# A cosine-gated MLP behind normalised linear attention: second batch's kv in one block on 128 partitions, leftover rows in 32-column tiles, g as a row, a new order

## The chip, the cores and the metric

The kernel runs on one core of one Trainium2 chip. The time is device time of one launch, in microseconds; three launches were timed and the median is used. One further execution was recorded by the hardware profiler, and the profile and trace come from it. The engines are TensorE (PE, matmuls), VectorE (DVE), ScalarE (ACT), GpSimd (POOL) and SyncE (SP, which here only issues DMAs).

## The reference

```python
# q, k, v: (8 batches, 8 heads, 576, 64); w_in: (512, 2048), w_out: (2048, 512) in float64
kv  = np.einsum('bhsd,bhse->bhde', k, v)
out = np.einsum('bhsd,bhde->bhse', q, kv)
rms = np.sqrt(np.mean(out * out, axis=-1, keepdims=True) + 1e-06)
x   = (out / rms * g_norm)          # then to (4608 tokens, 512): heads side by side
h   = x @ w_in
g   = h * np.cos(h)
y   = (g @ w_out).astype(np.float32)
```

The attention has no softmax, so each head's k and v shrink to one 64x64 matrix kv, and each token's q is multiplied by it. The bulk of the work is the two matrix products of the MLP.

## The kernel before

**Chunks and steps.** The 4608 tokens are cut into nine chunks of 512. A batch has 576 tokens, so the second chunk (c = 1) holds the last 64 tokens of batch 0, the "leftover rows", and 448 of batch 1. The inner width of 2048 is cut into 16 pieces j. A step is a chunk and a j: stage 1 (`stage1_part`) makes h for 128 of the 2048 columns, `act_part` makes g from it on ACT and DVE, stage 2 (`stage2_part`) adds g times a piece of w_out to four accumulators. Stage 1 takes the four head pairs p = 0 to 3 of x in this order, three matmuls for each. Every fp32 value is split into a high and a low part (`xhi`, `xlo`; `ghi`, `glo`; the two halves of a weight tile), and three products stand for one; so a step has 12 matmuls of 128x512 in stage 1 and 12 in stage 2, and there are 9 x 16 = 144 steps. The first steps alternate between the first two chunks (`segments`, line 256), so that each weight is used twice soon after its arrival: steps 0 to 3 are chunk 0, 4 to 11 chunk 1.

**Weights.** `w_loads` (line 429) fetches a piece of w_in or w_out as 64-bit words, 512 KB each; `w_part` (line 698) turns it into two fp32 tiles with two or three ACT and three or four DVE operations.

**The front.** The first two batches (`FRONT = 2`) have a path of their own. `kv_loads_front` (line 376) loads k and v of one pair of heads: for batch 0 as 64 rows per head, both heads on 128 partitions, for batch 1 on 96 partitions with six tokens each. `kv_front_part` (line 452) multiplies them on PE, one pair at a time, and copies the 64x64 results into the block-diagonal tile `kv_front`. `q_loads_front` (line 410) loads q of one pair; `x_front_part` (line 531) transposes it on PE, multiplies it by `kv_front`, squares (ACT), sums (DVE), takes the power -0.5 on POOL, scales (DVE), transposes back on PE, and makes `xhi` (ACT, scaled by `gcol`, the column of g) and `xlo` (DVE). For chunk 1 each pair does six products (lines 558 to 563): four on 128 rows of batch 1, of which the first two cover rows that are not batch 1's, and two of 32 columns that overwrite those rows with the leftover rows of batch 0. Later batches use `kv_part` (line 494): all four pairs in one block, with four full tiles of 128 tokens and the last 64 tokens (`k_over`, `v_over`, zero-filled to 128) as a fifth product.

**g.** Line 391 loads g as a column of 64 partitions, four bytes each, on ACT's queue; `g_part` (line 354) copies it to the other 64.

**The order.** A planner written out in the kernel (`Order`, line 52) sets the order on every engine. Each piece of work is a generator that waits for events, takes tokens (buffers) and asks for time on an engine with a cost and a priority. The planner walks through time and takes the piece that can start first, and among those the one with the lowest priority value; `keep_in_program_order` fixes what comes out. The priorities are due times, `due(i) = 24 + 5.4 i + 2 min(i, 11)`, shifted by a table `haste` (line 274). Loads are such pieces on an engine "DMA" (`load`, line 339), and their order is the order in which SP issues them.

**Borrowed memory.** The front's tiles use the names of weight tiles (`lend`, line 889), so in the trace a front load of k reads `wi<-in_k_dram` or `wo<-in_k_dram`, and a kv product `bank<-wo,wi`. The products of q are `acc<-wo,m` (chunk 0) and `bank<-wo,m` (chunk 1). The weights whose tiles are lent wait for the release.

**Start-up.** Lines 240 and 241 issue 34 matmuls on a tile of zeros, before any data has come.

All engine instructions but a few carry line 207 in the trace, since they go through the `Pinned` helper; so they are told apart by their tiles.

Of the kernel before, what the change touches and what calls it, by code (L numbers as in the profile page):

```python
# [51 lines left out]
class Order:  # L52
# [23 lines left out]
    def advance(self, proc, value):  # L76
        while True:
            try:
                req = proc.gen.send(value)
            except StopIteration:  # L80
                self.live.discard(proc)
                return
            value = None
            self.seq += 1
            if req[0] == "run":
                proc.shape = req[3] if len(req) > 3 else None
                self.pending.append((req[2], self.seq, proc.t, req[1], proc))
                return
            if req[0] == "wait":
                proc.t = max([proc.t] + [e.t for e in req[1] if e.t is not None])  # L90
                proc.left = [e for e in req[1] if e.t is None]
                if proc.left:
                    for e in proc.left:
                        e.waiters.append(proc)
                    return
            else:
                tokens = req[1]
                if not tokens.free:
                    heapq.heappush(tokens.waiters, (req[2] if len(req) > 2 else -100.0, self.seq, proc))
# [27 lines left out]
    def run(self):  # L127
        while self.pending:
# [15 lines left out]
            if e == "PE":  # L144

                d = (2 * d if start < 6 else d) + (self.CHANGE if proc.shape != self.shape else 0)
                self.shape = proc.shape
# [7 lines left out]
def tile_kernel(  # L155
# [25 lines left out]

    FRONT = 2
    SF = 2 * S // P
    SP = 96
    SQ = S // SP

# [10 lines left out]
    sched.busy["DMA"] = 1.0  # L197
# [42 lines left out]
    for _ in range(34):  # L240
        pe.matmul(out=bank[:, 0:P], lhsT=zeros, rhs=zeros, start=True, stop=True)
    ident = const.tile([P, P], F32, name="ident")
# [8 lines left out]
    for t in (k_over, v_over):  # L251
        pool.memset(t[ST:P], 0.0)
    gcol = const.tile([P, 1], F32, name="gcol")
# [15 lines left out]
    def due(i):  # L269
# [14 lines left out]
        ("act", 16): 16.2, ("act", 29): 32.0, ("act", 35): 63.7, ("act", 4): -10, ("act", 5): -8.1,  # L284
        ("act", 8): 10.6, ("acc", 0): 28.7, ("acc", 1): 19.9, ("acc", 10): 20.7, ("acc", 13): 59.2,
        ("acc", 14): 44.4, ("acc", 18): 32.3, ("acc", 26): 10.6, ("acc", 28): 15.6, ("acc", 33): 25.2,
        ("acc", 46): 5.6, ("acc", 53): 6.8, ("acc", 8): 12.3, ("xd", 2, 0): -3.8, ("xd", 2, 2): -11.8,
        ("xd", 2, 3): -24.5, ("xd", 3, 0): -12.5,
# [33 lines left out]
    g_in, over_in = Event(), events(B)  # L322
# [28 lines left out]
    def load_g():  # L351
        pass

    def g_part():
        yield "wait", [g_in]
        yield "run", [("ACT", 0.1)], -11.0
        act.copy(out=gcol[D:2 * D, :], in_=gcol[0:D, :])

# [16 lines left out]

    def kv_loads_front(b, p, tags):

        def issue():
            shape = [P, 2, SQ, D] if b else [P, SF, D]
            kv_tiles[b, p] = [wpool.tile(shape, F32, name=f"{kind}{j}") for kind, j in tags]  # L380
            for t, src in zip(kv_tiles[b, p], (k, v)):
                heads = src[b, 2 * p:2 * p + 2]

                queue = nc.sync if b or p else act
                if b:
                    queue.dma_start(out=t[0:SP], in_=heads.rearrange("h (p i) d -> p h i d", i=SQ))  # L386
                else:
                    queue.dma_start(out=t, in_=heads.rearrange("h (p i) d -> (h p) i d", i=SF))
            if not b and not p:
                act.activation(out=warm, in_=warm, func=AF.Sin)  # L390
                act.dma_start(out=gcol[0:D, :], in_=g_norm.rearrange("(d o) -> d o", o=1))
# [18 lines left out]
    def q_loads_front(c, p, tag):  # L410

        def issue():
            if tag not in q_fronts:
                q_fronts[tag] = wpool.tile([P, 4, NTT, D], F32, name=f"{tag[0]}{tag[1]}")
            qn = q_fronts[tag][:, 2 * (p % 2):2 * (p % 2) + 2, :, :]
            heads = slice(2 * p, 2 * p + 2)
# [9 lines left out]
            q_tiles[c, p] = qn  # L426
# [25 lines left out]
    def kv_front_part(b, p, prio):  # L452
# [4 lines left out]
        _, end = yield "run", [("PE", 0.7 if b else 1.05)], prio, D if b else 0  # L457
# [3 lines left out]
        n = SQ if b else SF  # L461
        for i in range(n):
            for j, r in enumerate(heads):
                lhs, rhs = (t[0:SP, j, i, :] if b else t[r, i, :] for t in (kt, vt))
                pe.matmul(out=ps[r, 0:D], lhsT=lhs, rhs=rhs, start=(i == 0), stop=(i == n - 1))
        sched.fire(kv_used[b, p], end)
        done = [Event(), Event()]

# [24 lines left out]

    def kv_part(b, prio):
# [6 lines left out]
        ps = ps_tile(bank)[:, 0:NP * D].rearrange("p (n d) -> p n d", d=D)  # L501
        heads = [slice(j * D, (j + 1) * D) for j in range(2)]
        for p in range(NP):
            kt, vt = kv_tiles.pop((b, p))
            for i in range(SI + 1):
                for j, r in enumerate(heads):
                    lhs, rhs = (
                        (kt[:, j, i, :], vt[:, j, i, :]) if i < SI else (t[:, 2 * p + j, :] for t in (k_over, v_over)))
                    pe.matmul(out=ps[r, p, :], lhsT=lhs, rhs=rhs, start=(i == 0), stop=(i == SI))
            sched.fire(kv_used[b, p], end)  # L510
            sched.give(t_two, end)
        end = yield from kv_parts(b, [ps[r] for r in heads], prio)
# [18 lines left out]
    def x_front_part(c, p, prio):  # L531
# [14 lines left out]
        todo = front_rows(c)  # L546
        yield "wait", [kv_done[b, p] for b in {b for b, _, _, _ in todo}]
# [6 lines left out]
        _, end = yield "run", [("PE", 1.6 if c else 0.95)], prio  # L554
# [3 lines left out]
        for b, r0, r1, m in todo:  # L558
            for j in range(2):
                o = (2 * j + m) * P  # L560
                pe.matmul(
                    out=by_token[r0:r1, 2 * m:2 * m + 2, j, :], lhsT=qT[:, o + r0:o + r1],
                    rhs=kv_front[b][:, 2 * p + j, :], start=True, stop=True)
# [7 lines left out]
        def heads(t):  # L571
# [8 lines left out]
        yield "run", [("POOL", 1.4)], prio  # L580
# [7 lines left out]
            in1=rinv.rearrange("p (n o) -> p n o", o=1).broadcast_to([P, 2 * NTT, D]), op=ALU.mult)  # L588
        _, end = yield "run", [("PE", 0.5)], prio
        for a in range(NTT):  # L590
            pe.transpose(out=ps[:, a * P:(a + 1) * P], in_=x[:, a * P:(a + 1) * P], identity=ident)
        sched.give(t_r, end)
        tokens = x_tokens(c, p)
# [17 lines left out]
    def x_part(c, p, prio):  # L611
# [23 lines left out]
        _, end = yield "run", [("PE", sum(2 * max(0.11, (n + 32) / 2400) for _, _, _, n in parts))], -1.0  # L635
# [62 lines left out]
    def w_part(key, prio):  # L698
# [23 lines left out]
        yield "wait", [low_done]  # L722
        yield "run", [("DVE", 0.69)], prio
# [53 lines left out]
    def act_part(i, h, bank):  # L777
# [11 lines left out]
        sched.give(t_ki, end)  # L789

# [22 lines left out]
    def stage2_part():  # L813
        for i, (c, j, first, final) in enumerate(steps):
            yield "wait", [w_done["wo", j], g_done[i]]
            for t in range(NTT):
# [13 lines left out]
                if final:  # L830
                    sched.spawn(out_part(c, t, accs[t], j == NJ - 1, due(i + 3)), end + 0.1)
# [64 lines left out]
    for b in range(FRONT):  # L896
# [4 lines left out]
        (pool if b else dve).memset(kv_front[b], 0.0)  # L901
    for c in range(FRONT):
        for p in range(NP):
            t = due(begin[c]) - 32 + 3 * p if c else -100.0 + p
            t += put_off("load kv", c, p)
            load(2.4 if c else 1.9, t, [kv_in[c, p]], kv_loads_front(c, p, lend(2, [kv_used[c, p]])))
            if p in (0, 2):
                [key] = lend(1, [q_used[c, p], q_used[c, p + 1]])
            t += put_off("load q", c, p)
            load(1.1 if c else 0.85, t, [q_in[c, p]], q_loads_front(c, p, key))  # L910
            if c == 0 and p == 1:
                load(0.5, t, [g_in], load_g)
                sched.spawn(g_part())
    for c in range(FRONT):
        for p in range(NP):
            t = due(begin[c]) - 24 + 1 * p if c else -10.0 + 0.5 * p
            sched.spawn(kv_front_part(c, p, t + put_off("kv", c, p)))
            sched.spawn(x_front_part(c, p, t + put_off("x", c, p)))
    for key in sorted(need, key=lambda x: (need[x], x)):
        t = due(need[key]) - 14.0 + put_off("load", *key)  # L920
        load(1.5, t, [w_in[key]], w_loads(key), wait=lent.get(key, ()))
# [11 lines left out]
    for b in range(FRONT, B):  # L933
        i, _ = window(chunks_of(b)[0])
        begun = gates[max(i - LEAD, last_step[0] + 1)]
        load(0.8, due(i) - 6.0, [over_in[b,]], over_loads(b), wait=[begun] + ([kv_used[b - 1, NP - 1]] if b > FRONT else []))
# [44 lines left out]
```

## Time and profile before

| | |
|---|---|
| median of three runs | 860.79 us (859.9 to 862.53) |
| the profiled execution | 862.48 us, span 860.7 us |
| PE idle in the span | 9.9 us |
| main matmuls (128x512) | 3456 of 4458 records on PE |
| DMA moved | 59.52 MB; 47.19 MB read from HBM, 11.53 MB written |
| loads of batch 1's k and v | 8 of 288 KB |
| loads of chunk 1's q | 12 (128, 96 and 32 KB for each pair) |

The span runs from the first to the last instruction; the execution's own time also holds what lies around it. A row of the timeline gives start, length, engine, line, operation, out<-in by the program's names, the shape of the stationary operand and of the moving one, and the number of records merged into the row. A fp32 matmul leaves two records. "PEld" is the loading of the stationary operand, which runs beside the matmuls. A window row gives the busy time of the engines within a stretch.

### The profile page before, as it was taken

How to read it: one execution, taken by the hardware profiler on the slowest of the kernel's cores; microseconds unless marked ns; L12 is line 12 of the kernel's file. 1: busy time of each engine (PE TensorE's matmuls, PEld its weight loads, DVE VectorE, ACT ScalarE, POOL GpSimd, SP SyncE). 2: the span in 40 equal slices, each digit the busy share in tenths (PEclk: the TensorE clock that was granted, in tenths of full speed). 3: DMA queues.
4: the chain of work that ended last, by engine and by line, in shares of the span. 5: the costliest groups of instructions: out<-in, count | busy, mean ns of one | idle time of the engine just before them, and what ended most of it. 6: DMA issues, size and time to landing. Idle time of an engine off the chain costs nothing.

```text
span 860.7 us, 12112 instructions
## 1 busy us (share of the span) xinstructions
PE 850.8 (99%) x4458; PEld 705.5 (82%) x4458; DVE 651.4 (76%) x1053; ACT 556.7 (65%) x1059; POOL 103.7 (12%) x49
## 2 busy tenths in 40 slices
PE   8899999999999999999999999999999999999998
PEld 7688888888788888888888888888888888888886
DVE  4999988899987757886778667876778678864554
ACT  4788888667666556665666566756666666664443
POOL 3310000013122101111102101210111111110000
PEclk9999999999999999999999999999999999999999
DMA  8996020371403111400223020402000110010001
GB/s 298 265 398 201 2 85 25 108 199 25 111 13 97 26 62 22 113 13 13 65 52 82 1 74 12 115 9 62 13 13 13 47 28 1 1 38 12 1 0 50
DMA packets 104731, 59.52 MB, mean 69 GB/s; under 512 B 69728, under 2 KB 95072, under 8 KB 104672
## 3 DMA queue, kind: packets, MB, share of 16 engines
q1 hardware_dynamic: 104160, 58.02, 23.4%
q8 instruction: 35, 0.57, 0.3%
q10 hardware_dynamic: 512, 0.72, 0.2%
q14 instruction: 24, 0.20, 0.1%
HBM read 47.19 MB, written 11.53 MB: 68 GB/s over the span
## 4 chain that ended last, share of the span: by engine, by line
PE 95%; DMA 3%; SPq 1%; DVE 0%; issue 0%; ACT 0%; DVEq 0%
PE bank L207 50%; PE acc L207 45%; DMA wi<-in_v_dram 2%; DMA wo<-in_k_dram 1%; DVE r L207 0%; SPq L437 0%; SPq L386 0%; SPq L418 0%; ACT r L207 0%; DVE glo L207 0%; DVE slot L207 0%; ACT ki L207 0%; ACT slot L207 0%; DVEq L207 0%
## 5 line engine op out<-in xcount | busy, mean ns | idle before, releaser
L207 PE MATMUL acc<-wo,ghi 128*128 128x512 f32 x1152 | 355.7, 390 | 0.0
L207 PE MATMUL bank<-xhi,wi 128*128 128x512 f32 x1088 | 337.3, 391 | 0.1
L207 PEld LDWEIGHTS acc<-wo,ghi 128*128 128x128 f32 x1152 | 215.7, 188 | 45.2 <-DVE slot L207 0.4
L207 ACT ACTIVATE r<-r 128x512 f32<-128x512 f32 x288 | 181.3, 630 | 94.4 <-DVE r L207 92.0
L207 PEld LDWEIGHTS bank<-xhi,wi 128*128 128x128 f32 x1088 | 202.4, 188 | 41.6 <-DVE wi L207 0.4
L207 PE MATMUL acc<-wo,glo 128*128 128x512 f32 x576 | 224.5, 390 | 0.3 <-DVE glo L207 0.3
L207 PE MATMUL bank<-xlo,wi 128*128 128x512 f32 x544 | 212.1, 390 | 0.1
L207 POOL TENSOR_TENSOR rinv<-ms,mhalf 128x16 f32<-128x16 f32 (+1 forms) x36 | 99.2, 2756 | 651.5 <-DVE ms L207 651.5
L207 DVE SCALAR_TENSOR_TENSOR r<-ki,bank 128x512 f32<-128x512 int32 x144 | 98.7, 686 | 72.1 <-ACT ki L207 70.6
L207 ACT ACTIVATE ki<-bank 128x512 int32<-128x512 f32 x144 | 85.6, 595 | 90.3 <-PE bank L207 86.5
L207 DVE SCALAR_TENSOR_TENSOR r<-r,bank 128x512 f32<-128x512 f32 x144 | 98.3, 683 | 55.1 <-ACT r L207 54.4
L207 PEld LDWEIGHTS acc<-wo,glo 128*128 128x128 f32 x576 | 108.1, 188 | 23.3 <-DVE glo L207 0.7
L207 PEld LDWEIGHTS bank<-xlo,wi 128*128 128x128 f32 x544 | 102.1, 188 | 21.8 <-DVE xlo L207 0.6
L207 ACT CAST ghi<-r 128x512 fp32r<-128x512 f32 x144 | 89.1, 619 | 43.2 <-DVE r L207 40.8
L207 DVE TENSOR_TENSOR glo<-r,ghi 128x512 fp32r<-128x512 f32 x144 | 99.0, 688 | 23.6 <-ACT ghi L207 21.2
L207 DVE SCALAR_TENSOR_TENSOR r<-ki,r 128x512 f32<-128x512 int32 x144 | 98.6, 685 | 1.2
L207 DVE TENSOR_TENSOR slot<-bank,slot 64x512 f32<-64x512 f32 x56 | 38.5, 688 | 19.0 <-ACT slot L207 18.1
L207 ACT COPY slot<-bank 64x512 f32<-64x512 f32 x56 | 32.6, 581 | 21.1 <-PE bank L207 20.2
L207 ACT ACTIVATE slot<-acc 128x512 f32<-128x512 f32 (+1 forms) x39 | 22.5, 592 | 8.8 <-PE acc L207 7.6
L207 ACT COPY swp<-part 32x16 f32<-32x16 f32 x112 | 22.6, 202 | 7.5 <-DVE part L207 5.8
L207 DVE STREAM_TRANSPOSE slot<-rinv 128x512 f32<-128x512 f32 x28 | 19.8, 706 | 4.1 <-POOL rinv L207 4.0
L207 DVE SCALAR_TENSOR_TENSOR sg<-sg,m 128x512 int32<-128x512 int32 x32 | 21.7, 685 | 0.6 <-ACT sg L207 0.6
(94 smaller groups left out, 580.1 us busy)
## 6 DMA issues: line engine op xcount, KB each, us to landing
out_dram<-slot SPq DMA_DIRECT2D x35, 256.0 KB, 2.0
wo<-in_moe_w_out_dram SPq DMA_DIRECT2D x16, 512.0 KB, 8.4
wi<-in_moe_w_in_dram SPq DMA_DIRECT2D x16, 512.0 KB, 8.6
m<-in_k_dram SPq DMA_DIRECT2D x24, 256.0 KB, 3.8
sg<-in_v_dram SPq DMA_DIRECT2D x24, 256.0 KB, 4.4
part<-slot SPq DMA_DIRECT2D x8, 256.0 KB, 5.7
slot<-part SPq DMA_DIRECT2D x8, 256.0 KB, 3.5
qb<-in_q_dram SPq DMA_DIRECT2D x32, 48.0 KB, 2.3
```

Of the source, the lines that this page charges most:

```text
L207: return lambda *a, **kw: tc.keep_in_program_order(f(*a, **kw))
```

## The change

1. **Batch 1's kv** is made by a new part, `kv_batch_part`, once k and v of all four pairs and the leftover rows have come: 128 partitions with four tokens each, the last 64 tokens through `k_over` and `v_over` as in `kv_part`. The four copies are of 64 x 256. `kv_front_part` is left to batch 0.
2. **Chunk 1's products of q**: the first 128 rows are done in eight products of 32 columns (32 rows of the result each), the leftover rows with batch 0's kv and the other three tiles with batch 1's; the other 128 rows in two whole products. So nothing is overwritten.
3. **g** is loaded twice as one row, on SP, with a priority; one PE matmul against a 1x1 of the identity turns it into a column, which ACT copies. The casts of x wait for it.
4. **q of chunk 1** is loaded for two pairs at a time.
5. **The first loads** (k, v and q of pair 0, q of pair 1) are issued at once, outside the planner, whose DMA then starts at 4.8; costs in the planner are new (loads 1.5 and 1.36 instead of 2.4, 1.9 and 1.5; POOL 1.65 instead of 1.4; no double PE time before 6). `haste` is a new table with more entries, and more keys (`kc`, `xn`, `xt`, `wb`, `ag`, `out`) shift priorities within a part. Priorities are rounded to thousandths.
6. **40 start-up matmuls** instead of 34.

```diff
-    for _ in range(34):
+    for _ in range(40):
         pe.matmul(out=bank[:, 0:P], lhsT=zeros, rhs=zeros, start=True, stop=True)
...
-        ("load kv", 0, 0): -15.1, ("load kv", 0, 1): 6.2, ("load kv", 0, 2): 2.5, ("load kv", 0, 3): 3.5,
-        ("load kv", 1, 1): -98.4, ("load kv", 1, 3): 27.5, ("load q", 0, 0): -4.0, ("load q", 0, 1): -28.8,
...
+        ("load kv", 0, 0): -15.1, ("load kv", 0, 1): -32.7, ("load kv", 0, 2): -615.2, ("load kv", 0, 3): -234.6,
+        ("load kv", 1, 0): -254.1, ("load kv", 1, 1): -98.4, ("load kv", 1, 2): -36.0, ("load q", 0, 0): -4.0,
+        ("load q", 0, 1): -28.8, ("load q", 0, 2): -682.5, ("load q", 0, 3): -16.6, ("load q", 1, 0): 209.1,
+        ("load q", 1, 2): 118.1, ("load q", 1, 3): -94.8, ("load", "wi", 0): -465.8, ("load", "wi", 1): -214.2,
...
+        ("load", "wi", 6): 50.8, ("load", "wi", 7): -26.1, ("load", "wo", 0): 10.0, ("load", "wo", 1): -295.7,
...
+    def load_g():
+        for j in range(2):
+            nc.sync.dma_start(out=grow[:, j, :], in_=g_norm.rearrange("(o d) -> o d", o=1))
+
+    def g_part(prio):
...
+        pe.matmul(
+            out=ps[:, 0:1], lhsT=grow.rearrange("o j d -> o (j d)"), rhs=ident[0:1, 0:1], start=True, stop=True)
+        _, end = yield "run", [("ACT", 0.2)], prio
+        act.copy(out=gcol, in_=ps[:, 0:1])
...
-            shape = [P, 2, SQ, D] if b else [P, SF, D]
+            shape = [P, 2, SI, D] if b else [P, SF, D]
...
-                    queue.dma_start(out=t[0:SP], in_=heads.rearrange("h (p i) d -> p h i d", i=SQ))
+                    queue.dma_start(out=t, in_=heads[:, 0:SI * P].rearrange("h (p i) d -> p h i d", i=SI))
...
+            n = 4 if c else 2
+            qn = q_fronts[tag][:, 2 * (p % 2):2 * (p % 2) + n, :, :]
+            heads = slice(2 * p, 2 * p + n)
...
+    def kv_batch_part(b, prio):
+
+        yield "wait", [kv_in[b, p] for p in range(NP)] + [over_in[b,]]
+        yield "take", t_psa, prio
+        bank = yield "take", t_bank, prio
+        _, end = yield "run", [("PE", 0.58 * NP)], prio, D
+        ps = kv_products(b, bank, end)
...
+        def copies(n):
+            j, r = n // 2, halves[n % 2]
+            e, end = yield "run", [("ACT", act_us(NP * D), 0.0), ("DVE", dve_us(NP * D), 0.3)], prio
+            copy(e, front[r, :, j, r], ps[halves[j]])
+            sched.fire(done[n], end)
...
-        todo = front_rows(c)
-        yield "wait", [kv_done[b, p] for b in {b for b, _, _, _ in todo}]
+
+        todo = [(0, P, m, j, c) for m in range(c, 2) for j in range(2)]
+        if c:
+
+
+            n = (S - CH) // 2
+            todo = [(r, r + n, 0, j, c if r else 0) for j in range(2) for r in range(0, P, n)] + todo
+        prio += put_off("xn", c, p)
+        yield "wait", [kv_done[b, p] for b in range(c + 1)]
...
+    at_once = {("kv", 0, 0): 6.8, ("q", 0, 0): 5.2, ("q", 0, 1): 6.8}
...
+                load(1.5, t, [kv_in[c, p]], issue)
+                if c and not p:
+                    load(1.6, t + put_off("load over"), [over_in[c,]], over_loads(c))
```

`kv_products` is the loop of products of `kv_part`, taken out so that both parts call it.

More of the change, by code (lines that the diff above doesn't have):

```diff
@@ L144, in run @@
             if e == "PE":
-                d = (2 * d if start < 6 else d) + (self.CHANGE if proc.shape != self.shape else 0)
+                d += self.CHANGE if proc.shape != self.shape else 0
                 self.shape = proc.shape
@@ L196, in tile_kernel @@
     sched = Order()
-    sched.busy["DMA"] = 1.0
+    sched.busy["DMA"] = 4.8
     class Pinned:
@@ L349, in load @@
         sched.spawn(part())
[L351 to L357, printed above, removed]
     def two(shape, dtype, which):
@@ L425, in issue @@
                         in_=q[b, heads, t:t + 2 * (r1 - r0), :].rearrange("h (r a) d -> r h a d", a=2))
-            q_tiles[c, p] = qn
+            for i in range(0, n, 2):
+                q_tiles[c, p + i // 2] = qn[:, i:i + 2]
         return issue
@@ L456, in kv_front_part @@
         bank = yield "take", t_bank, prio
-        _, end = yield "run", [("PE", 0.7 if b else 1.05)], prio, D if b else 0
+        _, end = yield "run", [("PE", 1.05)], prio, 0
         ps = ps_tile(bank)
@@ L460, in kv_front_part @@
         heads = [slice(j * D, (j + 1) * D) for j in range(2)]
[L461 to L465, printed above, removed]
+        for i in range(SF):
+            for r in heads:
+                pe.matmul(out=ps[r, 0:D], lhsT=kt[r, i, :], rhs=vt[r, i, :], start=(i == 0), stop=(i == SF - 1))
         sched.fire(kv_used[b, p], end)
         done = [Event(), Event()]
+        prio += put_off("kc", b, p)
         def copies(j):
@@ L492, in kv_parts, with kv_products @@
         return end
+    halves = [slice(j * D, (j + 1) * D) for j in range(2)]
+    def kv_products(b, bank, end):
+        ps = ps_tile(bank)[:, 0:NP * D].rearrange("p (n d) -> p n d", d=D)
+        for p in range(NP):
+            kt, vt = kv_tiles.pop((b, p))
+            for i in range(SI + 1):
+                for j, r in enumerate(halves):
+                    lhs, rhs = (
+                        (kt[:, j, i, :], vt[:, j, i, :]) if i < SI else (t[:, 2 * p + j, :] for t in (k_over, v_over)))
+                    pe.matmul(out=ps[r, p, :], lhsT=lhs, rhs=rhs, start=(i == 0), stop=(i == SI))
+            sched.fire(kv_used[b, p], end)
+        return ps
+    def kv_batch_part(b, prio):
+        yield "wait", [kv_in[b, p] for p in range(NP)] + [over_in[b,]]
+        yield "take", t_psa, prio
+        bank = yield "take", t_bank, prio
+        _, end = yield "run", [("PE", 0.58 * NP)], prio, D
+        ps = kv_products(b, bank, end)
+        prio += put_off("kc", b, 0)
+        front = kv_front[b].rearrange("p (n j) d -> p n j d", j=2)
+        done = [Event() for _ in range(4)]
+        def copies(n):
[3 more added lines that the diff above has]
+            sched.fire(done[n], end)
+        for n in range(4):
+            sched.spawn(copies(n), end)
+        yield "wait", done
+        end = max(e.t for e in done)
+        give_ps(bank, end)
+        for p in range(NP):
+            sched.fire(kv_done[b, p], end)
     def kv_part(b, prio):
@@ L500, in kv_part @@
         _, end = yield "run", [("PE", 0.58 * NP)], -1.0, D
[L501 to L510, printed above, removed]
+        ps = kv_products(b, bank, end)
+        for _ in range(NP):
             sched.give(t_two, end)
-        end = yield from kv_parts(b, [ps[r] for r in heads], prio)
+        end = yield from kv_parts(b, [ps[r] for r in halves], prio)
         give_ps(bank, end)
@@ L553, in x_front_part @@
             bank = yield "take", t_bank, prio
-        _, end = yield "run", [("PE", 1.6 if c else 0.95)], prio
+        _, end = yield "run", [("PE", 1.25 if c else 0.95)], prio
         ps = ps_o.tile([P, DM], F32, name=f"acc{acc}") if c == 0 else ps_tile(bank)
         by_token = ps.rearrange("p (a j d) -> p a j d", j=2, d=D)
[L558 to L563, printed above, removed]
+        for r0, r1, m, j, b in todo:
+            o = (2 * j + m) * P
+            pe.matmul(
+                out=by_token[r0:r1, 2 * m:2 * m + 2, j, :], lhsT=qT[:, o + r0:o + r1],
+                rhs=kv_front[b][:, 2 * p + j, :], start=True, stop=True)
         sched.fire(q_used[c, p], end)
@@ L634, in x_part @@
             banks.append((yield "take", t_bank, prio))
-        _, end = yield "run", [("PE", sum(2 * max(0.11, (n + 32) / 2400) for _, _, _, n in parts))], -1.0
+        _, end = yield "run", [("PE", 0.05 + sum(2 * (n + 30) / 2400 for _, _, _, n in parts))], -1.0
         both = [ps_tile(bank) for bank in banks]
@@ L905, in tile_kernel @@
             t += put_off("load kv", c, p)
-            load(2.4 if c else 1.9, t, [kv_in[c, p]], kv_loads_front(c, p, lend(2, [kv_used[c, p]])))
+            issue = kv_loads_front(c, p, lend(2, [kv_used[c, p]]))
+            if ("kv", c, p) in at_once:
+                issue()
+                sched.fire(kv_in[c, p], at_once["kv", c, p])
+            else:
+                load(1.5, t, [kv_in[c, p]], issue)
+                if c and not p:
+                    load(1.6, t + put_off("load over"), [over_in[c,]], over_loads(c))
             if p in (0, 2):
                 [key] = lend(1, [q_used[c, p], q_used[c, p + 1]])
+            if c and p % 2:
+                continue
             t += put_off("load q", c, p)
[L910 to L913, printed above, removed]
+            issue = q_loads_front(c, p, key)
+            if ("q", c, p) in at_once:
+                issue()
+                sched.fire(q_in[c, p], at_once["q", c, p])
+            else:
+                load(1.7 if c else 0.68, t, [q_in[c, p + i] for i in range(c + 1)], issue)
+    act.activation(out=warm, in_=warm, func=AF.Sin)
+    load(0.1, -90.0 + put_off("load g"), [g_in], load_g)
+    sched.spawn(g_part(-11.0 + put_off("g")))
     for c in range(FRONT):
@@ L920, in tile_kernel @@
         t = due(need[key]) - 14.0 + put_off("load", *key)
-        load(1.5, t, [w_in[key]], w_loads(key), wait=lent.get(key, ()))
+        load(1.36 if need[key] < 5 else 1.3, t, [w_in[key]], w_loads(key), wait=lent.get(key, ()))
         sched.spawn(w_part(key, due(need[key]) - 0.0 + put_off(*key)))
@@ L935, in tile_kernel @@
         begun = gates[max(i - LEAD, last_step[0] + 1)]
-        load(0.8, due(i) - 6.0, [over_in[b,]], over_loads(b), wait=[begun] + ([kv_used[b - 1, NP - 1]] if b > FRONT else []))
+        load(0.8, due(i) - 6.0, [over_in[b,]], over_loads(b), wait=[begun, kv_used[b - 1, NP - 1]])
         for p in range(NP):
```

49 lines of the change are left out of this document (31 added, 18 removed), and 22 rows, old and new, of the table haste.

## The prediction

> **What bounds the kernel now.** I read the page first, then the windows by stage, then PE's timeline of the first 45 us, and last the DMA side of the same stretch.
>
> ```profile
> span 860.7 us, 12112 instructions
> PE 850.8 (99%) x4458; PEld 705.5 (82%) x4458; DVE 651.4 (76%) x1053; ACT 556.7 (65%) x1059; POOL 103.7 (12%) x49
> ...
> L207 PE MATMUL acc<-wo,ghi 128*128 128x512 f32 x1152 | 355.7, 390 | 0.0
> ```
> ```profile
> 20.00:30.00 10.00, 8.65 (x96) 6.82 (x95) 9.52 (x18) 8.62 (x21) 3.24 (x2) 1.00 1.07 295
> ...
> 50.00:60.00 10.00, 10.00 (x49) 8.22 (x49) 9.18 (x17) 8.18 (x14) 2.56 (x2) 1.00 1.06 398
> 60.00:80.00 20.00, 20.00 (x90) 16.57 (x89) 18.80 (x32) 17.68 (x33) 0.00 (x0) 1.00 0.82 244
> ...
> 800.00:861.00 61.00, 57.01 (x252) 46.81 (x250) 29.66 (x44) 27.07 (x45) 0.00 (x0) 0.99 0.05 18
> ```
>
> A window row gives the stretch, its length, then busy time of PE, PEld, DVE, ACT and POOL, the granted clock, the DMA share and GB/s. PE lacks 9.9 us of the span: 4.0 of them in the last window (the last result on its way out) and nearly all the rest before 45 us. A busy PE is not a PE at its peak, so the pace has to be read too; the chain of waits gives it.
>
> ```profile
> 63.96 5.44 PE acc L207 x24
> ```
>
> 24 matmuls in 5.44 us is 0.227 us each, and the 144 steps have 24 each: 3456 x 0.227 = 783 us that this change does not touch. From 45 us on PE is a full queue: what is taken out of PE's work shortens the span one for one, and what another engine saves there is worth nothing. Before 45 us PE waits, and the order decides.
>
> ```profile
> 7.79 2.19 PE L207 MATMUL bank<-wo,wi 64*64 64x64 f32 x36
> ...
> 11.87 1.26 PE L207 MATMUL bank<-wi,wo 64*64 64x64 f32 x36
> ...
> 15.23 1.16 PE L207 MATMUL acc<-wo,m 128*128 128x128 f32 x8 [1.51 <-DVE m L207]
> ...
> 17.42 1.22 PE L207 MATMUL bank<-wo,wo 64*64 64x64 f32 x36
> ...
> 19.06 1.95 PE L207 MATMUL acc<-wo,m 128*128 128x128 f32 x16
> 20.84 0.60 PE L207 MATMUL acc<-ident,r 128*128 128x128 f32 x4
> ...
> 21.81 0.92 PE L207 MATMUL bank<-wi,wo 96*64 96x64 f32 x24
> 22.66 0.66 PE L207 MATMUL bank<-ident,wi 128*128 128x128 f32 x4
> 24.44 0.63 PE L207 MATMUL acc<-ident,r 128*128 128x128 f32 x4 [1.13 <-DVE r L207]
> 24.91 1.61 PE L207 MATMUL bank<-wo,m 128*128 128x128 f32 x12
> 26.45 0.66 PE L207 MATMUL acc<-ident,r 128*128 128x128 f32 x4
> ...
> 27.88 1.09 PE L207 MATMUL bank<-xhi,wi 128*128 128x512 f32 x2
> ...
> 29.04 0.63 PE L207 MATMUL bank<-xhi,wi 128*128 128x512 f32 x2
> ...
> 32.44 0.92 PE L207 MATMUL bank<-wi,wo 96*64 96x64 f32 x24 [0.75 <-DMA wi<-in_v_dram]
> ```
>
> These rows are start, length, instruction and, in brackets, the wait. The four waits that matter are 1.51, 1.13, 0.75 and one of 0.47 ahead of the last group of 96 rows at 42.07 (its row stands below): 3.9 us. The first stage-1 matmuls come at 27.88 and those of head pair 1 at 29.04.
>
> **The change part by part.** Every duration is of the profiled execution: 862.48 us with a span of 860.7, so 1.8 us lie around the span. The three timed runs have their median at 860.79. I keep the outside at its size and put the difference on the median.
>
> *The second batch's kv on PE.* It was four groups of 24 records of 96 rows; a fp32 matmul leaves two records. One group holds PE from 21.81 to 22.66, 0.85 us; four are 3.40. The new form is that of the later batches, on 128 rows with the leftover rows as a fifth accumulation:
>
> ```profile
> 42.07 0.92 PE L207 MATMUL bank<-wo,wi 96*64 96x64 f32 x24 [0.47 <-issue]
> ```
> ```profile
> 399.55 0.39 PE L207 MATMUL bank<-xlo,wi 128*128 128x512 f32 x1
> 399.87 0.69 PE L207 MATMUL bank<-sg,m 128*64 128x64 f32 x16
> ...
> 402.35 0.73 PE L207 MATMUL acc<-wo,ghi 128*128 128x512 f32 x2
> ```
>
> That is 80 records from 399.87 to 402.35: 2.48 us. Entering the form costs 0.32 - 0.227 = 0.09 us (399.55 to 399.87), now once instead of four times. Gain 0.92 + 0.28 = **1.2 us**; bounds 0.9 (the entries lie in waits) and 1.3.
>
> *The leftover rows of x.* Each pair of the second chunk had 12 records from 24.91 to 26.45, 1.54 us. Whole ones cost 0.111 us (16 from 19.06 to 20.84), so the eight whole ones take 0.89 and the four on 32 columns 0.65: 0.44 of work and 0.2 for two changes of form. The new part has four whole records (0.44), sixteen on 32 columns and the same changes (0.2). If the four column tiles run side by side, sixteen cost 4 x 0.11 = 0.44 and the part 1.09; two at a time, 1.5; one after another, 2.4. Over four pairs that is 1.8 us gained, nothing, or 3.4 lost. The nearest rows are the 64-column ones: 24 records in 0.85 us, 0.035 each, while half of a 0.111 record is 0.055, so two do run side by side. I take between two and four: 1.25 a part, **1.2 us** gained.
>
> *g as a row.* It adds one matmul of one column and an ACT copy, in a form of its own: **0.2 us** lost (0 to 0.4). The 64 four-byte pieces become two rows. But all casts of x now wait for g, and its load is put tenth in the queue; it was among the first. What queues behind such a cast on ACT and DVE are the weights' conversions and later pairs; stage 1 waits for them.
>
> *Copies of kv.* Sixteen of 64x64 for the second batch become four of 64x256:
>
> ```profile
> L207 ACT COPY wo<-bank 64x64 f32<-64x64 f32 x24 | 4.9, 206 | 2.8 <-PE bank L207 2.6
> ...
> L207 ACT CAST kv_w<-bank 64x256 fp32r<-64x256 f32 x24 | 8.8, 368 | 6.9 <-PE bank L207 6.6
> ```
>
> 16 x 0.206 = 3.3 us against 4 x 0.37 = 1.5. ACT and DVE gain 1.8 us at a time when DVE is 95% busy (20 to 30 us). I count it as nothing, since PE's queue covers it; without that cover it is worth up to 1.8.
>
> *The loads.* The second batch on 128 partitions, and q of two pairs in one go (12 loads become 6).
>
> ```profile
> 5.00:13.70 8.70, 8.03 (x96) 6.61 (x96) 2.59 (x6) 3.44 (x8) 0.23 (x1) 1.00 1.04 393
> 13.70:32.30 18.60, 15.13 (x193) 12.44 (x192) 16.08 (x34) 13.55 (x34) 7.94 (x5) 1.00 1.00 273
> ...
> 18.00:20.00 2.00, 2.00 (x35) 1.93 (x32) 0.75 (x3) 1.57 (x6) 1.64 (x1) 1.00 0.64 156
> ```
> ```profile
> 12.85 2.41 SPq L423 DMA_DIRECT2D wi<-in_q_dram  x3
> 17.54 0.39 SPq L437 DMA_DIRECT2D wi<-in_moe_w_in_dram  x1
> ```
> ```profile
> k_over<-in_k_dram SPq DMA_DIRECT2D x6, 128.0 KB, 2.9
> ```
>
> The stretch with the 96-row loads moves 273 GB/s with the engines full, the one before it 393; and where q's small pieces hold SP (12.85 to 17.54 without another issue) the rate falls to 156. Both causes go. Two loads of leftover rows come in, 128 KB each; the same loads later take 2.9 us from issue to landing. All of it runs beside PE; the first 45 us feel it through the waits.
> The Trainium skill ("DMA: Bandwidth & Descriptors", Specifications) asks for at least 512 bytes per piece for line rate. The leftover rows are 256 bytes, which speaks against this part; by the row above the two loads may hold the queue some 2 us, and only the batch's own kv and what is queued behind it would feel that.
>
> *The order.* The load priorities can be worked out from the diff's table. After kv and q of pair 0 and q of pair 1 come q2, kv2, wi0, q3, kv3, wo1, the second batch's first kv, wi1, and only then **kv of pair 1**, with g behind it; before, pair 1's kv was the last of the first batch but ahead of all weights save one. Up to pair 1's kv that is 4288 KB.
>
> ```profile
> 2.74 6.52 DMA wo<-in_k_dram
> ```
>
> This load lands at 9.26, and with it 2144 KB in all, by the order of issue; the new order's 1088 KB of the start would so be in at about 6.5. Another 4288 KB (4.39 MB) at 393 GB/s end at 17.7, at 273 at 22.6. From pair 1's kv at 17.42 to its first stage-1 matmul at 29.04 it took 11.6 us; the same distance gives 29.3 now. So head pair 1 is not earlier. What gains is what lies ahead of it: wi0 is loaded third after the start instead of ninth, so pair 0's matmuls of three steps (9 x 0.227 = 2.0 us) can fill the waits of 1.51 and 1.13, and the wait for in_v (0.75) goes with the faster queue. What is late next is pair 1. I take half of the 3.9 us, **1.9 gained**; bounds: all 3.9, or 5 lost (rival 3).
>
> The six more start-up matmuls run while PE has nothing else, and cost nothing; of the clock, see rival 1.
>
> Sum: -1.2 - 1.2 + 0.2 - 1.9 = -4.1; 860.8 - 4.1 = **856.7 us**.
>
> **The rivals.**
> 1. *The front pays in full.*
>
> ```profile
> 0.98 3.81 PE L207 MATMUL bank<-zeros 128*128 128x128 bf16 x34 [0.98 <-DVE zeros L207]
> 5.28 1.08 PE L207 MATMUL bank<-ident,wi 128*128 128x128 f32 x4 [0.48 <-POOL wo L207]
> ```
>
> The first 36-record group takes 2.19 us, the next 1.26, though the window rows give the clock as 1.00 there: PE is slow up to about 10 us. If 40 start-up matmuls in place of 34 close the gap of 0.48 ahead of 5.28 and the group is fast from the start, 0.9 us go, and with all 3.9 of the waits: -2.2 - 3.9 - 0.9 = -7.0, **853.8**. For it: the waits have named causes that the change touches. Against it: pair 1's place. The Trainium skill ("TensorE: Matmul & The Clock Gate", Part 1) gives full clock after a busy window of about 3.4 us that runs freely; by that rule six more matmuls help in some executions and not in others.
> 2. *The gain on PE turns into waiting.* Pair 1 and g come as late as before, PE runs out of pair 0's matmuls, and 2 us of new waits stand where the work was: **860.6**. DVE at 92 to 95% from 20 to 60 us speaks for it; that PE never waits after 45 us speaks against it.
> 3. *Slower: pair 1's kv is late.* If the queue keeps 273 GB/s, it lands at 22.6 instead of 17.7, and stage 1, which takes the pairs in order, stops 4.9 us at pair 1 in all open steps: -4.1 + 1.9 + 4.9 = +2.7, and with g's casts behind it up to +4: **864**. It decides from a landing at about 22 us on. Against it: 393 GB/s hold in the two stretches without 96-row loads (5 to 13.7; 50 to 60 with 398).
> 4. *The column tiles do not overlap*, so the change does not do on PE what it says: 3.4 lost where 1.2 was gained: 861.3.
>
> **How the numbers follow.** Chances: forecast 0.47 (854.5 to 858.5), rival 1 0.17, rival 2 0.20, rival 3 0.11, rival 4 0.05. A measurement of this kernel tells 0.3% apart, 2.6 us: faster is below 858.2, slower above 863.4. Faster: 0.44 of the forecast and rival 1, some of rival 2's edge: 0.63. Slower: rival 3 and an edge of 4: 0.12. Between: 0.25. The range 852.5 to 862 leaves out most of rival 3 and the best of rival 1.
>
> **What would show it.** PE's groups of 96 rows gone, and one block of 80 records of about 2.5 us near 30 us; x's groups of the second chunk at 20 records in 1.1 to 1.5 us (2.4 is rival 4); GB/s near 390 from 13 to 32 us; pair 0's stage-1 matmuls before 25 us; pair 1's near 29 (34 is rival 3). PE's first windows show the waits that are left. The forecast is wrong if PE waits again after 45 us, as DVE has the same work for a shorter time.

## The result, and the profile after

| | before | after |
|---|---|---|
| median of the timed runs | 860.47 us (859.9 to 862.53, 7 runs) | 865.79 us (863.3 to 866.14, 7 runs) |
| the profiled execution | 862.48 us, span 860.7 | 865.56 us, span 863.8 |
| span less PE's busy time | 9.9 us | 15.1 us |

The ratio is 1.0054, 95% interval 1.0041 to 1.0067: the change made the kernel slower by 4.6 us (3.5 to 5.8; the medians lie 5.3 us apart). The forecast was 856.7 us. The time is close to the 864 of rival 3.

From the page of after, the first lines (span; busy time of the engines; in the second part the slices of 21.6 us each with busy tenths, the clock and the rate):

```profile
span 863.8 us, 12145 instructions
...
PE 848.7 (98%) x4482; PEld 703.7 (81%) x4482; DVE 651.2 (75%) x1051; ACT 553.8 (64%) x1049; POOL 104.0 (12%) x49
...
PE   7799999999999999999999999999999999999998
...
PEclk9899999999999999999999999999999999999999
```

PE works 2.1 us less than before (850.8), and the span is 3.1 us longer: 5.2 us of idle time have come in. They are spread over the first three slices (by windows of a slice's length 1.6, 2.4 and 1.6 us more than before); the largest part is in the second, and there the clock is low too. The window rows of after show where (columns as in the prediction: start and end, length, busy time of PE, PEld, DVE, ACT and POOL with instruction counts, clock, DMA share, GB/s):

```profile
5.00:13.70 8.70, 7.63 (x141) 6.71 (x139) 3.45 (x10) 4.31 (x11) 0.22 (x1) 1.00 1.04 376
13.70:32.30 18.60, 10.76 (x87) 8.99 (x88) 14.58 (x27) 12.40 (x28) 7.68 (x4) 0.82 1.10 334
...
24.00:26.00 2.00, 0.00 (x0) 0.00 (x0) 2.00 (x5) 0.72 (x2) 1.44 (x1) 0.81 1.14 305
26.00:28.00 2.00, 0.32 (x2) 0.35 (x3) 1.06 (x3) 1.71 (x3) 0.57 (x1) 0.50 1.11 355
28.00:30.00 2.00, 2.00 (x10) 1.90 (x9) 1.77 (x3) 0.93 (x2) 0.00 (x0) 0.50 0.95 344
30.00:32.00 2.00, 2.00 (x7) 1.41 (x6) 0.69 (x1) 0.76 (x2) 0.00 (x0) 0.50 1.05 396
32.00:34.00 2.00, 2.00 (x53) 1.83 (x53) 0.61 (x1) 1.33 (x3) 0.00 (x0) 0.98 1.06 395
```

From 13.7 to 32.3 us PE is busy 10.76 of 18.6 us; before it was 15.13. The DMA queue is not the reason in general: it moves 334 GB/s there, against 273 before. PE's timeline of after names the wait:

```profile
16.71 0.61 PE L206 MATMUL acc<-ident,r 128*128 128x128 f32 x4
18.95 1.26 PE L206 MATMUL bank<-wo,wo 64*64 64x64 f32 x36 [1.63 <-DMA wo<-in_v_dram]
20.14 0.38 PE L206 MATMUL bank<-ident,grow 1*128 1x1 f32 x2
20.45 0.66 PE L206 MATMUL acc<-ident,r 128*128 128x128 f32 x4
...
22.13 0.60 PE L206 MATMUL acc<-ident,r 128*128 128x128 f32 x4
27.68 1.94 PE L206 MATMUL bank<-ident,wi 128*128 128x128 f32 x8 [4.95 <-DMA wi<-in_q_dram]
29.27 1.20 PE L206 MATMUL bank<-xhi,wi 128*128 128x512 f32 x2
...
32.56 0.69 PE L206 MATMUL bank<-wo,wi 128*64 128x64 f32 x16
...
34.83 0.29 PE L206 MATMUL bank<-v_over,k_over 128*64 128x64 f32 x4
35.05 0.73 PE L206 MATMUL bank<-xhi,wi 128*128 128x512 f32 x2
...
37.32 1.29 PE L206 MATMUL bank<-wo,m 128*32 128x128 f32 x20
38.36 0.70 PE L206 MATMUL bank<-xhi,wi 128*128 128x512 f32 x2
...
45.03 1.29 PE L206 MATMUL bank<-wo,m 128*32 128x128 f32 x20 [1.07 <-DVE r L206]
```

At 22.7 us PE has nothing left that stands ahead of the transposes of the second chunk's q in its fixed order. That q comes at 27.55; PE stands 4.95 us, and by then both of pair 0's casts are done. The rows of ACT and of DVE:

```profile
24.04 0.69 ACT L206 ACTIVATE xhi<-acc,gcol 128x512 fp32r<-128x512 f32 x1
```
```profile
25.60 0.74 DVE L206 SCALAR_TENSOR_TENSOR xlo<-acc,gcol,xhi 128x512 fp32r<-128x512 f32 x1
```

So the high part of pair 0's x is there from 24.73 on and the low part from 26.34: of the wait for q, the first 2 us had nothing of pair 0 to fill them either. The first stage-1 matmul comes at 29.27 (27.88 before) and needs 1.20 us for two where 35.05 has 0.73: it runs at the clock of 0.50. The batch's kv follows from 32.56 to 35.05, and pair 1's first stage-1 matmul at 35.05 (29.04 before). The longest wait after that is 1.07 us for DVE, just ahead of 45.03.

The chain of waits of after says since when q was on its way:

```profile
14.45 6.39 DMA wi<-in_moe_w_in_dram
20.84 0.02 issue
20.86 6.69 DMA wi<-in_q_dram
27.55 0.14 issue
27.68 4.50 PE bank L206 x14
```

q's last piece goes out at 20.86, when the weight issued at 14.45 has landed, and takes 6.69 us: by the trace's order of issue and landing the leftover rows, pair 1 of batch 1's k and v and one more weight (1280 KB) are all still ahead of it.

### The profile page after: what moved, and what is told of

Read it like the earlier page. It is cut to its first block, busy times and chain, and to the rows that moved or that the text cites. A ratio compares the mean times of both kernels' runs of the same rounds, so it can differ in the third digit from the quotient of the medians.

```text
span 863.8 us, 12145 instructions
## 1 busy us (share of the span) xinstructions
PE 848.7 (98%) x4482; PEld 703.7 (81%) x4482; DVE 651.2 (75%) x1051; ACT 553.8 (64%) x1049; POOL 104.0 (12%) x49
## 4 chain that ended last, share of the span: by engine, by line
PE 95%; DMA 3%; DVE 1%; POOL 1%; ACT 0%; issue 0%; SPq 0%; POOLq 0%
PE bank L206 50%; PE acc L206 45%; DMA wi<-in_q_dram 1%; DMA wo<-in_moe_w_out_dram 1%; DMA wi<-in_moe_w_in_dram 1%; POOL rinv L206 1%; DVE r L206 0%; DVE ms L206 0%; ACT slot L206 0%; DVE xlo L206 0%; DVE glo L206 0%; DVE wi L206 0%; DVE sg L206 0%; SPq L446 0%; DVE slot L206 0%
## 5 line engine op out<-in xcount | busy, mean ns | idle before, releaser
L206 DVE SCALAR_TENSOR_TENSOR r<-r,bank 128x512 f32<-128x512 f32 x144 | 98.0, 681 | 44.9 <-ACT r L206 44.2
L206 ACT COPY swp<-part 32x16 f32<-32x16 f32 x112 | 22.6, 202 | 10.3 <-DVE part L206 8.6
L206 ACT ACTIVATE slot<-acc 128x512 f32<-128x512 f32 (+1 forms) x39 | 22.7, 592 | 6.1 <-PE acc L206 5.0
L206 DVE TENSOR_TENSOR m<-qT,m 64x512 fp32r<-64x512 f32 x28 | 19.2, 685 | 5.2 <-ACT m L206 4.5
```

The costliest lines, as they stand in the source:

```text
L206: return lambda *a, **kw: tc.keep_in_program_order(f(*a, **kw))
```

## The experiments

Theory 1: the two edits on PE save what they should, and **the new order** loses more than that in the first 50 us. Theory 2: one thing does the harm, either q's place in the queue, or the clock, or g. Kernels with names in a_ are the kernel after with one edit, those in b_ are the kernel before with one part of the change. Each is compared with the kernel before, timed in the same rounds.

### The edits on PE alone, in the old order

**b_tiles**: the column tiles alone.

```diff
-        for b, r0, r1, m in todo:
-            for j in range(2):
...
+        tiles = [(0, P, m, j, c) for m in range(c, 2) for j in range(2)]
+        if c:
+            n = (S - CH) // 2
+            tiles = [(r, r + n, 0, j, c if r else 0) for j in range(2) for r in range(0, P, n)] + tiles
+        for r0, r1, m, j, b in tiles:
```

> The kernel before with the column tiles alone: in the four parts of the second chunk eight products of 32 columns and two whole ones instead of four whole ones and two of 32 columns; orders unchanged. Theory A (PE sets the time; four column tiles run side by side): each part takes 1.05 us instead of 1.54, the time falls by 2.0 us, to 858.5. Theory B (two of the four parts lie in the first 45 us, where PE waits anyway): half of it, 1.0 us.

Measured: 860.0 us against 860.86, ratio 0.9986 (0.9973 to 0.9998). The part takes 1.04 us in after (37.32 to 38.36) instead of 1.54: 2.0 us of work less, of which 1.2 (0.2 to 2.3) reach the time.

**b_kv128**: batch 1's k and v on 128 partitions, the leftover rows as a fifth product, still pair by pair, the leftover rows loaded with pair 1.

```diff
-                    queue.dma_start(out=t[0:SP], in_=heads.rearrange("h (p i) d -> p h i d", i=SQ))
+                    queue.dma_start(out=t, in_=heads[:, 0:SI * P].rearrange("h (p i) d -> p h i d", i=SI))
...
+            if (b, p) == (1, 1):
+                over_loads(b)()
```

> The kernel before with the second batch's k and v on 128 partitions and the leftover rows as a fifth product, but still pair by pair and in the order of before; the leftover rows are loaded with the first of these pairs. Theory A (the 96-row loads slow the whole DMA queue): the stretch from 13.7 to 32.3 us moves about 350 GB/s instead of 273, the waits for in_v at 32.4 go, and the last of these loads lands about 4 us earlier than 42; the time falls by 0.5 to 1 us, since PE's waits on loads before 45 us are only 1.2 us. Theory B (the rate is low for another cause, q's 512-byte pieces or the full queue): rate and time stay.

Measured: 860.48 against 861.36, ratio 0.999 (0.9982 to 0.9999). Two window rows of b_kv128:

```profile
13.70:32.30 18.60, 15.84 (x206) 13.05 (x206) 15.84 (x31) 13.63 (x34) 7.13 (x5) 1.00 0.98 284
...
32.30:42.00 9.70, 9.70 (x71) 7.83 (x70) 8.49 (x17) 7.50 (x17) 1.64 (x1) 1.00 1.03 355
```

In the stretch that the prediction read as slowed by the 96-row loads the rate goes from 273 to 284 GB/s only. In the next one, where the last two pairs are loaded, it goes from 249 to 355. But b_tiles and b_zeros40, which keep the 96-row loads, have 292 and 285 GB/s in the first of these stretches and 336 and 328 in the second: the profiled execution of before was low in both, and no gain in rate is shown for the 128 rows. (The leftover rows' small pieces come in with them, so the run does not isolate the 96 rows either.) PE still waits 1.23 us for a v ahead of 31.08.

**b_both**: both edits, as in the two diffs above, on the old order.

> The kernel before with both: column tiles and 128 partitions, orders unchanged. If the two gains add up: 0.9 us of the tiles (as the run of the tiles alone had it) and 0.5 to 1 us of the loads, 1.4 to 1.9 us in all, about 859. If the tiles' other half lies in waits that the loads end: 2.5 us, 858.4.

Measured: 859.66 us (859.25 to 860.65, 11 runs), ratio 0.9981 (0.9972 to 0.9989). This is faster than both kernels: 1.6 us below before, 6.1 below after. Its page, beside that of after, gives the balance:

```profile
span 857.8 us, 12145 instructions
...
PE 847.1 (99%) x4474; PEld 700.8 (82%) x4474; DVE 650.8 (76%) x1053; ACT 556.4 (65%) x1059; POOL 103.7 (12%) x49
```

Both kernels have the tiles and the 128-row kv. After has a span 6.0 us longer: 4.4 us of it idle (15.1 against 10.7) and 1.6 busy. The busy part is mainly the clock: PE works from 27.68 to about 32.1 us at half speed, some 2.2 us lost. So what remains of the change besides these two edits (the order, the loads of q for two pairs, g as a row, kv in one block, the start-up) loses 6 us. From 23 to 50 us alone PE idles 6.0 us in after and 1.4 in b_both. No run takes the loads for two pairs or the one block of kv apart from the order.

**b_zeros40**: before with 40 start-up matmuls.

```diff
-    for _ in range(34):
+    for _ in range(40):
```

> The kernel before with 40 start-up matmuls instead of 34. If the gap of 0.48 us ahead of the first transposes keeps PE slow to about 10 us: the first group of 36 records takes 1.26 us instead of 2.19, and the time falls by 0 to 1 us, since PE waits for its loads a little later. Rival: the clock comes up when it does, whatever stands in the gap, and the group still takes 2.19 us.

Measured: 860.49, ratio 0.9995 (0.9983 to 1.0007): no difference. In its profiled execution the first 36-record group takes 1.26 us, but the same group takes 1.26 in that of b_tiles with 34 matmuls. The 2.19 in the profile of before was a matter of that execution, so the balance with b_both above is safer than one with before.

### Keeping the clock up

**a_warm**: after, with 80 matmuls on zeros ahead of the q transposes that wait.

```diff
+        for _ in range(80 if (c, p) == (1, 1) else 0):
+            pe.matmul(out=ps_t[:, 0:P], lhsT=zeros, rhs=zeros, start=True, stop=True)
```

> The changed kernel with 80 matmuls on zeros put on PE ahead of the two transposes of the second chunk that wait 4.95 us for q; nothing else moves. Theory A (the wait itself and the halved clock after it make the change slower): PE is busy from 22.7 to 27.5, the granted clock stays 1.00 through 26 to 32 us instead of 0.50, the stretch of 4.5 us after the wait (27.68 to 32.18) shrinks to about 2.3, and the time falls by 2 us or a little more, to about 863.5. Theory B (DVE and ACT, which make x, set the end there, and the clock is a side effect): the clock stays up, the time stays at 865.8.

Measured: 865.14 (863.01 to 866.34, 6 runs), ratio 1.0044 (1.0027 to 1.0062). PE's timeline of a_warm:

```profile
22.52 4.63 PE L206 MATMUL bank<-zeros 128*128 128x128 bf16 x80
26.98 1.04 PE L206 MATMUL bank<-ident,wi 128*128 128x128 f32 x8
27.78 0.71 PE L206 MATMUL bank<-xhi,wi 128*128 128x512 f32 x2
...
32.27 0.73 PE L206 MATMUL bank<-xhi,wi 128*128 128x512 f32 x2
```

The stretch is at full pace: from the q transposes to pair 1's stage 1 it takes 5.29 us instead of 7.37 (27.68 to 35.05), and pair 1 begins 2.8 us earlier. In the executions whose clock was 1.00 throughout the time was 863.0 and 863.7, about 2 us below after's median; in the other four (864.8 to 866.3) the mean clock was 0.995 to 0.998, so it fell somewhere; where, no trace shows. After itself has one execution of 863.3, with a mean clock of 0.998, and six of 865.6 to 866.1 with 0.994 to 0.996. The low clock is real and costs about 2 us, but with it gone the kernel is still 2.2 to 2.9 us slower than before in the same rounds (860.86).

### Moving one thing

**a_q_early**: after, with only SP's order changed: q of pairs 0 and 1 ahead of the leftover rows and pair 1 of batch 1's kv. The loads that stood ahead are held back until q is out.

```diff
-            issue()
+            if late:
+                held.append(issue)
+            else:
+                issue()
+                while last and held:
+                    held.pop(0)()
```

> The changed kernel with one difference in SP's order: q of pairs 0 and 1 of the second chunk is issued ahead of the leftover rows and of k and v of pair 1; PE, DVE and ACT keep their orders. Theory A: q lands near 23.7 instead of 27.55, PE waits about 1 us for it and then some 1.7 us for pair 0's low part, which is ready at 26.3; the clock does not drop; the time falls by about 4 us, to 861.5. Theory B (x of pair 0 and pair 1 come when they come): the wait only changes its name and the time stays within 1 us of 865.8.

Measured: 866.06 (864.88 to 867.61, 6 runs), ratio 1.0054 (1.0038 to 1.007). From PE's timeline of a_q_early:

```profile
24.50 1.06 PE L206 MATMUL bank<-ident,wi 128*128 128x128 f32 x8 [1.43 <-DMA wi<-in_q_dram]
...
31.13 0.73 PE L206 MATMUL bank<-xhi,wi 128*128 128x512 f32 x2
...
46.16 1.08 PE L206 MATMUL bank<-ident,wo 128*128 128x128 f32 x4 [3.15 <-DMA wo<-in_q_dram]
46.89 1.20 PE L206 MATMUL acc<-wo,ghi 128*128 128x512 f32 x2
```

The wait goes from 4.95 to 1.43 and pair 1 begins at 31.13 instead of 35.05, 3.9 us earlier. All of it is given back at 46 us: PE waits 3.15 us for the q of pairs 2 and 3, whose transposes begin at 46.16 (46.15 in after), and the clock goes to 0.50 there (47 to 49 us), as the 1.20 us for two matmuls shows.

**a_q_both**: after, with both loads of q moved up, the second to ahead of the first piece of w_out.

```diff
+            if c:
+                before_it["over" if p == 0 else ("wo", 0)] = [issue]
+                issue = lambda: None
```

> The changed kernel with both of the second chunk's q loads issued earlier on SP: q of pairs 0 and 1 ahead of the leftover rows, q of pairs 2 and 3 ahead of the weight wo0; all orders on PE, DVE and ACT stay. In the run with the first of the two alone, PE waited 3.15 us near 46 for the second and the clock fell there. Theory A (what PE lacks is q, and each long wait also halves the clock): no wait over 2 us is left before 60 us, the clock stays up in most executions, the time falls to 861.5 to 863. Theory B (DVE has the same work to do and is behind by then, 2.00 of 2.00 us busy from 40 to 46): the wait turns into one for DVE near 43 us and the time stays above 864.

Measured: 865.83 (864.43 to 865.92, 5 runs), ratio 1.0042 (1.0027 to 1.0057). Both waits for q are gone. PE's timeline and then ACT's of a_q_both:

```profile
22.64 1.06 PE L206 MATMUL bank<-ident,wi 128*128 128x128 f32 x8
...
29.14 1.22 PE L206 MATMUL bank<-xhi,wi 128*128 128x512 f32 x2 [2.76 <-ACT m L206]
...
35.35 0.74 PE L206 MATMUL bank<-xhi,wi 128*128 128x512 f32 x2
```
```profile
23.52 0.70 ACT L206 ACTIVATE xhi<-acc,gcol 128x512 fp32r<-128x512 f32 x1
26.89 0.66 ACT L206 ACTIVATE sg<-wo 128x512 f32<-128x512 f32 x1 [2.67 <-DMA wo<-in_moe_w_out_dram]
...
28.50 1.07 ACT L206 COPY m<-bank 128x512 f32<-128x512 f32 x2
```

q is in time, but the weight that was ahead of it is not. ACT waits 2.67 us for that weight, since the weight's conversion stands next in ACT's order, and behind it stand the copies of the transposed q, the first of which ends PE's wait: PE waits 2.76 us, the clock falls, and pair 1 begins at 35.35. This wait is in neither of the two expectations.

**a_g_early**: after, with g loaded on ACT's queue behind pair 0's k and v, and its matmul right behind the start-up ones.

```diff
+    for j in range(2):
+        act.dma_start(out=grow[:, j, :], in_=g_norm.rearrange("(o d) -> o d", o=1))
+    pe.matmul(out=bank0[:, 0:1], lhsT=grow.rearrange("o j d -> o (j d)"), rhs=ident[0:1, 0:1], start=True, stop=True)
+    act.copy(out=gcol, in_=bank0[:, 0:1])
```

> The kernel after, with one edit: g is loaded on ACT's queue ahead of everything but pair 0's k and v, and its matmul and ACT copy stand right behind the start-up matmuls, as early as in the kernel before; all other orders are those of after. Theory A (the order on PE and the place of the loads hold the front up, not g): the first cast of x (ACT m, 21.33 in after) moves by less than 1 us, since ACT's copies of pair 1's kv (20.25 and 20.88) stand ahead of it in ACT's order, PE still waits about 5 us for q at 22.7, and the time is 865.2 to 866.2 (after: 865.8). Theory B (the casts are late because they wait for g): the first casts move to about 17.5 to 18.5, pair 1's stage 1 from 35.05 to about 32, and the time falls by 2 us or more, to 863.8 or less. The early matmul may also hold up PE's first transposes if g lands after 5 us; then the first group of 36 records starts later than 5.55.

Measured: 868.7 (867.58 to 869.6, 5 runs), ratio 1.0084 (1.007 to 1.0098). PE's timeline, then ACT's and DVE's, of a_g_early:

```profile
6.56 0.35 PE L206 MATMUL bank<-ident,grow 1*128 1x1 f32 x2 [1.79 <-DMA grow<-in_g_norm_dram]
6.83 0.69 PE L206 MATMUL bank<-ident,wi 128*128 128x128 f32 x4
7.46 2.19 PE L206 MATMUL bank<-wo,wi 64*64 64x64 f32 x36
...
27.50 1.67 PE L206 MATMUL bank<-ident,wi 128*128 128x128 f32 x8 [3.36 <-DMA wi<-in_q_dram]
...
34.40 0.73 PE L206 MATMUL bank<-xhi,wi 128*128 128x512 f32 x2
...
45.50 1.09 PE L206 MATMUL bank<-ident,r 128*128 128x128 f32 x4 [2.74 <-DVE r L206]
```
```profile
21.29 0.69 ACT L206 ACTIVATE m<-acc,gcol 128x512 fp32r<-128x512 f32 x1
```
```profile
42.03 0.43 DVE L206 TENSOR_SCALAR m<-wi 128x512 int32<-128x512 uint32 x1 [2.73 <-DMA wi<-in_moe_w_in_dram]
```

The place that I chose for g holds up PE's start by 1.79 us, and the first group then runs at the slow pace. That is made up by pair 1, which begins at 34.40 (35.05 in after). The time is worse than either theory expected because of what comes later: DVE stands 2.73 us for a weight that is next in its order, PE then 2.74 us for DVE, and the clock is at 0.50 from 44.9 to 51.7 us. On the question the run says this much: the first cast of x is at 21.29 although g has been there since 7 us (21.33 in after). In the order of after the casts do not wait for g when they run. They stand behind ACT's copies of pair 1's kv, and these behind the load that lands at 18.86. But this order was planned with g where it is, and the run keeps it: no cast stands ahead of the copy of g at 20.70, though pair 0's x was transposed by 17.3. Whether an order planned with an early g would cast sooner was not run.

### What follows

Theory 1 holds, in this form. The edits save time in the old order; what is left of the change loses more, and the loss is seen as waits and a low clock before 50 us. In the new order each engine's order (PE, ACT, DVE, SP) is fixed to a plan in which pair 1, the weights and the second chunk's q arrive one just behind the other. The planner of the changed kernel, worked through by itself, has q of pairs 0 and 1 in at 25.94 us and leaves PE without work from 22.84 to 25.94; that is a plan, not a measurement. On the chip q came 1.6 us later than that, and the clock, of which the planner knows nothing, fell. Moving one load moved the wait to the next load or to the next piece in ACT's order, twice, at the same time in the end (865.8 and 866.1, against 865.8); in a_g_early it came back for a weight in DVE's order. Theory 2 falls for q and for the clock as single causes, and for g as long as the order stays; the clock is a part of about 2 us.

Open: whether a table searched anew with a price on idle stretches would make the whole change pay was not tried. From 38.6 to 50 us the chain of waits of after runs over ACT, DVE and POOL and no longer over loads (DVE is busy 9.68 of 10 us from 40 to 50), so DVE's order may hold up what is left once the loads are in time; no run tests that. The rate dips to 180 GB/s from 18 to 20 us in after, and from 22 to 24 us (156) in a_q_early; which of the loads makes the dip, the small pieces of the leftover rows or another, the runs do not settle.

## Why the prediction was wrong, step by step

- **What bounds the kernel.** Right: PE's queue from 45 us on, the order before. All that went wrong lies before 50 us.
- **The second batch's kv on PE.** The block takes 2.49 us (32.56 to 35.05), 2.48 was forecast.
- **The leftover rows of x.** 1.25 us for a part was taken, between two and four tiles at a time; it is 1.04. With 0.44 for the whole ones and 0.2 for the changes of form, about 0.40 is left for the sixteen records. In the trace of after they begin four at a time, the four within 0.02 us of each other: all four column tiles run side by side. Rival 4 is out, and the end of the range that the prediction would not take was the right one.
- **Of the two together** 1.6 us reach the time in the old order (0.9 to 2.4), where the prediction took 2.4. The interval holds both a loss of part of the gain to waits ahead of 45 us and no loss at all, so whether work taken out of PE's queue shortens the span one for one is not settled.
- **g as a row.** 0.2 forecast, 0.31 on PE (20.14 to 20.45). What the prediction feared of it, casts that wait for g, does not occur when the kernel runs, as a_g_early shows; that the order itself was planned around a late g is not excluded.
- **Copies of kv.** Counted as nothing; no run contradicts it or isolates it.
- **The loads.** 390 GB/s forecast from 13 to 32 us, 334 measured. The cause that the prediction gave for the 273 of before, 96-row loads, is not borne out (284 with 128 rows in b_kv128, 285 and 292 with 96 rows in b_zeros40 and b_tiles). The Trainium skill ("DMA: Bandwidth & Descriptors", Specifications) speaks against the pieces of 256 bytes; the dip to 180 GB/s fits it, but the runs do not show that these pieces make it.
- **The order: the step that failed.** It was a gain of 1.9 us; in its place stands most of the 6.0 us that after loses on b_both (PE's idle time from 23 to 50 us, 6.0 against 1.4, and 2.2 us of low clock). Pair 1's kv was forecast in at 17.7 and landed at 18.86, so its load was judged nearly right. The error was in the next sentence: that from there to stage 1 "the same distance", 11.6 us, would do, and that pair 0's matmuls would fill the waits. It took 16.1 us (18.95 to 35.05). PE does not take what is ready; it takes what is next, and next, ahead of pair 0's first stage-1 matmul, stood the transposes of a load that the prediction had not followed. Nor could pair 0's matmuls have filled the waits, since its x came late: it was transposed by 17.3 but cast only from 24.04 to 26.34, behind other work in the orders of ACT and DVE (from 19.26 in before). The prediction listed the queue up to pair 1's kv and stopped there. Carried on past a weight, the leftover rows, a pair of batch 1's k and v and another weight, q of the second chunk ends 2304 KB (2.36 MB) later, at 327 GB/s, the rate of 20 to 30 us, 7.2 us behind pair 1's kv; it was 8.7 (18.86 to 27.55). Whether PE's order has work ahead of it was not to be read from the diff, but its being open was a reason to give this term a wider bound.
- **The clock.** The prediction weighed it for the start alone (rival 1). A wait of 5 us inside the kernel brought it down again, for 2.2 us more.
- **Rival 3** gave 864 for a kernel whose pair 1 comes at 34. Pair 1 came at 35.05 and the time is 865.8. Its consequence was right; its cause, a queue at 273 GB/s with pair 1's kv in at 22.6, was not, so that the time fits is luck. It had 0.11. Rival 2, waits in place of work, named pair 1 and g as the late ones, and was 5 us too small; of the signs read for and against it, DVE was busy 90 to 95% and not 92 to 95% from 20 to 60 us, and PE had one wait of 0.3 us after 45. Rival 1's fast first group appeared (1.26 us), but b_tiles has it with 34 matmuls too.

## What to carry to other kernels

Where a change replaces a whole order, follow every load past the one that looks critical until the first main matmul of each chunk has its data, and ask of each engine what stands in line ahead of it; an engine with a fixed order waits for what is next, not for what it could do. Judge edits of work and a new order apart: here the edits in the old order gave 0.9981 (0.9972 to 0.9989), and with the new order and the rest of the change 1.0054. Here a wait on PE of 2.7 to 5 us brought the clock down and so cost its length and up to about 2 us more, and a load moved to cure one wait is only a cure if nothing is fixed behind the loads that it passes.

## What the runs showed of the hardware

- After the wait of 4.95 us the granted clock was 0.50 from about 25.3 to 32.1 us, long after PE was busy again at 27.68. Waits of 3.15 us (a_q_early), 2.76 us with smaller ones ahead (a_q_both) and 2.74 us (a_g_early) brought it down too. The Trainium skill ("TensorE: Matmul & The Clock Gate", Part 1) gives free-running windows of 3413 ns: 6.83 us would be two of them, so the trace agrees, and that the same program loses clock in one execution and not in the next (a_warm) fits the free run.
- Four fp32 products on 32 columns each run fully side by side: in the trace of after sixteen records from 37.32 us on begin four at a time, each four 0.11 to 0.13 us after the last, while whole ones begin 0.11 us apart one by one.
- A row of g, two loads of 256 bytes, took 4.8 us from its first issue (1.80 us, ACT's queue) to PE's release (6.56 us) behind pair 0's loads: here the size of a load said little about when it landed.
